# w3 x w_out on merged words as native float32 products, and a planner that books GpSimd and VectorE together

## The chip, the core and the metric

The kernel runs on one NeuronCore of a Trainium2 chip. In the views PE is TensorE, PEld its weight load, DVE VectorE, ACT ScalarE, POOL GpSimd, and SP the engine that issues the DMAs. The metric is the device time of one execution in microseconds: the kernel before takes 945.75 us (median of 3 runs, 943.49 to 945.9). The profile comes from one execution of its own, of 944.89 us, with a span of 943.1 us from its first to its last instruction.

## The reference, cut to what matters

Attention over 4 batches, 8 heads, 576 positions and 64 columns a head, with a window of 128 positions and a slope for each head, feeds two dense layers over the 2304 tokens:

```
scores = where(0 <= i - j < 128, q @ k.T / 8 - slope * |i - j|, -1e9)
x = softmax(scores) @ v                     # 2304 x 512
x = ((x @ w1) * (x @ w2)) @ w3 @ w_out      # w1, w2: 512x1024; w3: 1024x1024; w_out: 1024x512
x = relu(x @ w_in) ** 2 @ w_out2            # w_in: 512x2048; w_out2: 2048x512
```

The activations are float32; all weights come as float64, as pairs of 32-bit words.

## The kernel before, in words

**Weights.** A weight tile is 128 rows of 1024 float64 numbers (1 MB), loaded by `w_load` (L253) into a tile `raw` of 128 x 1024 x 2 words. Four passes turn each pair into one float32 word that stands in the place of the low word: `conv_g` (L266) scales the high word, `conv_s` (L270) shifts the low one, and `conv_m` (L281, twice, on DVE alone) merges them. Two more passes split the merged word for TensorE: `conv_hi` (L288) copies it as fp32r, `conv_lo` (L299) subtracts the copy from the word; both halves go to a tile `wu`. A product of two such operands is `mm3` (L155): three fp32r products (high x high, high x low, low x high, L156 to L158). There are 36 tiles: 4 of w_out (`wo`), 8 of w3, 8 of w1 and w2 (`w12`) and 16 of the last layer (`w2`).

**W34.** Before any token passes, `p_w34` (L700) forms w3 x w_out in 64 steps (8 rows of blocks, 8 blocks of the inner sum each), each step one `mm3` of 128 x 512 from a w3 tile and half of a `wo` tile into PSUM tile `g`. `l_w34h` and `l_w34l` split the result. All 64 steps must be done before the tiles of the gated layer are opened (`gp`, L875).

**Heads.** A head (`add_head`, L603) goes through load, scaling or splitting of q and k, `p_qk` (ten score products, tile `s`), `l_min` (L406, DVE, from PSUM), `l_exp` (ACT), `l_sum` (DVE, small), `l_norm` (L439, any of three engines), transposes `p_tr1`, `p_tr2` (tile `t`), a copy of them (`l_pth`), and the product with v, `p_pva` and `p_pvb` (tiles `a`, `b`). Heads in `NQ` (the first 9) have native float32 score products, heads in `NV` (the first 12) native float32 products with v; the others take split operands. A native product of N columns runs as two passes over its N columns, which the views count as two instructions. Two heads make one 128-row block of x, split by `t_xh` and `t_xl` in two halves of 288 tokens.

**Gated layer.** For each batch and half, `p_ab` (L743) makes two up-projections of 12 products of 288 columns for each of 8 blocks; `l_a` (ACT) copies the first, `l_gf` (L756, DVE) multiplies by the second, `l_gh` and `l_gl` split the gate (tile `gt`). `p_y` multiplies by W34. All heads but those of the first batch are worked in between. The last layer follows after the planned part, in a fixed order (`r_step`, `o_step`, from L910).

**What sets the order.** `Plan.run` (L52) is a list scheduler. Each task has a rank, a price on each engine that can take it, what it waits for, and the buffers that it takes and gives back. The planner takes the earliest start and, among tasks that can start then, the lowest rank; a task goes to the engine where its end plus a bias (L37) is lowest. What it writes down is each engine's instruction order; on the chip every engine works through its own list in that order and waits by semaphores. In the kernel before, each engine is booked for itself.

## Time and profile before

| | |
|---|---|
| time, median of 3 runs | 945.75 us (943.49 to 945.9) |
| the profiled execution | 944.89 us, span 943.1 us |
| busy over the span | PE 905.7, DVE 470.6, ACT 420.5, POOL 325.9 us |
| until the first up-projection starts | 145.49 us |
| from there to the first product of the last layer | 394.3 us |
| the last layer | 403.3 us |

A matmul's duration in the views includes the time in which it runs through the array, so a busy PE is not the same as a full PE: what a product costs in a dense stretch is read from the distance between two starts. The views give an instruction's wall time, with the time in which it was held up after its start in it.

### The profile page before, as it was taken

What the parts mean: (1) busy time and instruction counts of PE and PEld (TensorE: products, weight loads), DVE (VectorE), ACT (ScalarE), POOL (GpSimd) and SP (SyncE); (2) the same over time, 40 slices, a digit from 0 to 9 for tenths busy, and PEclk for the clock granted to TensorE, in tenths of its full rate; (3) what the DMA queues carried; (4) which work ended last, traced back from release to release, by engine and by line L of the source; (5) the groups of instructions that cost most, each with busy time, mean ns of one, the idle gap of its engine ahead of it and who ended that gap; (6) DMA issues with size and microseconds to landing.
All of it is one profiled execution on the core that took longest, in us unless ns stands there. A gap on an engine that the chain in (4) does not pass through costs nothing.

```text
span 943.1 us, 13950 instructions
## 1 busy us (share of the span) xinstructions
PE 905.7 (96%) x5248; PEld 791.0 (84%) x5248; DVE 470.6 (50%) x981; ACT 420.5 (45%) x955; POOL 325.9 (35%) x354
## 2 busy tenths in 40 slices
PE   5699988999999999999999999999999999999998
PEld 3466657899999999999999978888888888888897
DVE  5969969667676665417313995231223122212222
ACT  4566667667777666434323353232223222222222
POOL 6887988766656655336323200000000000000000
PEclk9899999999999999999999999999999999999999
DMA  7647542233332322025006541020002000100010
GB/s 228 216 159 244 169 135 83 64 98 82 74 83 65 105 66 63 7 72 195 31 7 210 177 146 48 0 74 17 1 1 79 0 1 8 49 0 1 1 46 23
DMA packets 31075, 73.74 MB, mean 78 GB/s; under 512 B 5792, under 2 KB 14496, under 8 KB 26912
## 3 DMA queue, kind: packets, MB, share of 16 engines
q1 hardware_dynamic: 31008, 72.86, 25.2%
q8 instruction: 41, 0.67, 0.3%
q14 instruction: 26, 0.21, 0.1%
HBM read 63.41 MB, written 9.44 MB: 77 GB/s over the span
## 4 chain that ended last, share of the span: by engine, by line
PE 79%; DVE 10%; POOL 5%; issue 3%; DMA 2%; ACT 1%; SPq 0%; POOLq 0%; DVEq 0%; ACTq 0%
PE g L156 9%; PE g L158 9%; PE g L157 9%; PE o L157 7%; PE o L158 7%; PE o L156 7%; PE r L157 7%; PE r L158 7%; PE r L156 7%; DVE raw L283 5%; POOL e L197 2%; PE s L447 2%; PE s L450 1%; PE s L449 1%; PE t L470 1%
## 5 line engine op out<-in xcount | busy, mean ns | idle before, releaser
L921 ACT ACTIVATE t<-r 128x512 f32<-128x512 f32 (+1 forms) x80 | 44.4, 555 | 258.7 <-PE r L158 258.7
L923 DVE CAST rr<-s 128x512 fp32r<-128x512 f32 (+1 forms) x80 | 32.0, 400 | 250.9 <-ACT s L922 250.8
L156 PE MATMUL g<-x,wu 128*128 128x288 f32 x512 | 153.7, 300 | 0.6 <-DVE gf L758 0.6
L157 PE MATMUL g<-x,wu 128*128 128x288 f32 x512 | 151.8, 297 | 0.0
L158 PE MATMUL g<-x,wu 128*128 128x288 f32 x512 | 151.5, 296 | 0.0
L157 PE MATMUL r<-ys,wu 128*128 128x512 f32 (+1 forms) x320 | 118.9, 371 | 0.0
L158 PE MATMUL r<-ys,wu 128*128 128x512 f32 (+1 forms) x320 | 118.8, 371 | 0.0
L156 PE MATMUL r<-ys,wu 128*128 128x512 f32 (+1 forms) x320 | 118.6, 371 | 0.0
L157 PE MATMUL o<-wu,rr 128*128 128x512 f32 x288 | 113.3, 393 | 0.0
L156 PE MATMUL o<-wu,rr 128*128 128x512 f32 x288 | 112.9, 392 | 0.0
L158 PE MATMUL o<-wu,rr 128*128 128x512 f32 x288 | 112.8, 392 | 0.1
L283 DVE SCALAR_TENSOR_TENSOR raw<-raw 128x1024 uint32<-128x1024 uint32 x72 | 109.1, 1517 | 1.5 <-POOL raw L197 0.4
L156 PEld LDWEIGHTS g<-x,wu 128*128 128x128 f32 x512 | 96.9, 189 | 0.9 <-DVE gf L758 0.9
L157 PEld LDWEIGHTS g<-x,wu 128*128 128x128 f32 x512 | 97.5, 190 | 0.0
L158 PEld LDWEIGHTS g<-x,wu 128*128 128x128 f32 x512 | 97.3, 190 | 0.0
L164 POOL TENSOR_TENSOR gt<-gf,gt 128x288 fp32r<-128x288 f32 x61 | 57.9, 951 | 99.4 <-ACT gt L161 98.9
L197 POOL TENSOR_SCALAR e<-e,st 128x256 f32<-128x256 f32 (+1 forms) x115 | 76.9, 684 | 23.7 <-DVE st L437 14.5
L156 PE MATMUL g<-gt,wu 128*128 128x288 f32 x256 | 76.6, 299 | 0.5 <-DVE gf L758 0.5
L157 PE MATMUL g<-gt,wu 128*128 128x288 f32 x256 | 75.9, 296 | 1.0 <-POOL gt L164 1.0
L158 PE MATMUL g<-gt,wu 128*128 128x288 f32 x256 | 75.5, 295 | 0.0
L758 DVE TENSOR_TENSOR gf<-g,a_sb 128x288 f32<-128x288 f32 x64 | 29.1, 454 | 83.9 <-PE g L158 83.8
L156 PEld LDWEIGHTS r<-ys,wu 128*128 128x128 f32 x320 | 60.2, 188 | 11.6
(123 smaller groups left out, 1863.0 us busy)
## 6 DMA issues: line engine op xcount, KB each, us to landing
raw<-in_w2io_dram SPq DMA_DIRECT2D x16, 1024.0 KB, 4.9
qkraw<-in_qk_dram SPq DMA_DIRECT2D x46, 288.0 KB, 4.3
raw<-in_w3t_dram SPq DMA_DIRECT2D x8, 1024.0 KB, 7.5
raw<-in_w_dram SPq DMA_DIRECT2D x8, 1024.0 KB, 5.1
y_scr<-ye SPq DMA_DIRECT2D x32, 144.0 KB, 1.7
out_dram<-ob SPq DMA_DIRECT2D x18, 256.0 KB, 2.1
raw<-in_w_out_dram SPq DMA_DIRECT2D x4, 1024.0 KB, 6.2
yr<-y_scr SPq DMA_DIRECT2D x16, 256.0 KB, 2.8
```

What stands on the lines that cost most here:

```text
L156: nc.tensor.matmul(o, wh, xh, start=start, stop=False)
L157: nc.tensor.matmul(o, wh, xl, start=False, stop=False)
L158: nc.tensor.matmul(o, wl, xh, start=False, stop=stop)
L164: eng.tensor_tensor(out=o, in0=a, in1=b, op=ALU.subtract)
L197: nc.gpsimd.tensor_scalar(out=o, in0=i, scalar1=c, scalar2=1.0, op0=ALU.mult, op1=ALU.mult)
L283: nc.vector.scalar_tensor_tensor(out=low, in0=high, scalar=(3, 0x80000000)[part], in1=low, op0=(ALU.logical_shift_left, ALU.bitwise_and)[p ...
L447: nc.tensor.matmul(o, qb, d["kh"][:, k0:k1], start=True, stop=True)
L449: nc.tensor.matmul(o, qb, d["kh"][:, k0:k1], start=True, stop=False)
L450: nc.tensor.matmul(o, qb, d["kl"][:, k0:k1], start=False, stop=True)
L758: nc.vector.tensor_tensor(out=t, in0=ab.pop((b, hf, fi, 1)), in1=ab.pop((b, hf, fi, 2)), op=ALU.mult)
L921: nc.scalar.activation(out=t, in_=o, func=ACTF.Relu)
L923: nc.vector.tensor_copy(out=rr[:, 0, 0:n], in_=s)
```

## The change

1. The split of the 12 `wo` and w3 tiles goes: the new `add_words` has the load and the four passes that merge, and `add_weights` adds the split for `w12` and `w2` alone. `p_w34` multiplies the merged words themselves, where they stand (every second word of `raw`), as one native float32 product of 128 x 512 for three fp32r ones. The `wo` words are loaded into the pool `su`.
2. The planner knows a second name for DVE, `D`: work of DVE that reads two operands from SBUF, or copies or scales from SBUF to SBUF. `D` and POOL's work are booked one at a time (`lock`). Reads of PSUM and the small sums stay `d`.
3. `NV` goes from 12 heads to 7, ranks and biases have new numbers, and a start may be up to 0.1 later for a lower rank (`LOOK`).
4. The first w3 tile is loaded before the first `wo` tile, and four native products of 256 columns of constants stand at the head of TensorE's list (`p_warm`).

```diff
--- before.py
+++ after.py
 NQ = frozenset(range(9))
-NV = frozenset(range(12))
-RANK = dict(w34=6.0, h0=-4.0, w12=85.0, w12s=10.0, w12l=10.0)
+NV = frozenset(range(7))
+RANK = dict(w34=6.25, h0=-10.7, w12=37.2, w12s=7.96, w12l=9.7)
...
-    LOOK = 0.0
-    bias = dict(d=1.75, a=0.7, p=0.0)
+    LOOK = 0.1
+    bias = dict(d=3.0, D=0.34, a=0.3, p=0.0)
...
+        lock = 0.0
...
                 best = None
-                for e, w in where.items():
+                for q, w in where.items():
+                    e = q.lower()
                     t = max(t0, free.get(e, 0.0))
+                    if q in "Dp":
+                        t = max(t, lock)
                     for d in deps:
                         t = max(t, end[d] + (0.0 if on[d] == e else self.lat[on[d]]))
-                    key = t + w + self.bias.get(e, 0.0)
+                    key = t + w + self.bias.get(q, 0.0)
                     if best is None or (key, t) < best[:2]:
-                        best = (key, t, e, w)
+                        best = (key, t, q, w)
...
-            t, rank, n, e, w = min(near, key=lambda c: (c[1], c[0], c[2]))
+            t, rank, n, q, w = min(near, key=lambda c: (c[1], c[0], c[2]))
+            e = q.lower()
...
             fin = t + w
             end[n], on[n] = fin, e
-            free[e] = t + (w if e != "dma" else w)
+            free[e] = fin
+            if q in "Dp":
+                lock = fin
...
     def w_copy(n, ps=False):
-        return {"a": 0.2 + n * 0.00094, "d": 0.2 + n * (0.0011 if ps else 0.0006)}
-
-    def w_tt(n, engs="dp"):
-        w = {"d": 0.15 + n * 0.00106, "p": 0.22 + n * 0.0023}
+        return {"a": 0.2 + n * 0.00094, "d" if ps else "D": 0.2 + n * (0.0011 if ps else 0.0006)}
+
+    def w_tt(n, engs="Dp"):
+        w = {"d": 0.15 + n * 0.00106, "D": 0.15 + n * 0.00106, "p": 0.22 + n * 0.0023}
         return {e: w[e] for e in engs}
 
-    def w_ts(n, engs="dap"):
-        w = {"d": 0.16 + n * 0.00053, "a": 0.2 + n * 0.00094, "p": 0.35 + n * 0.0009}
+    def w_ts(n, engs="Dap"):
+        w = {"D": 0.16 + n * 0.00053, "a": 0.2 + n * 0.00094, "p": 0.35 + n * 0.0009}
         return {e: w[e] for e in engs}
 
...
     def w_load(key):
         kind, i = key
         src = {"wo": w_out, "w3": w3t, "w12": w12, "w2": w2io}[kind]
-        t = wp.tile([128, 1024, 2], U32, tag="u", bufs=10, name="raw")
+        if kind == "wo":
+            t = su.tile([128, 1024, 2], U32, tag="v", bufs=4, name="raw")
+        else:
+            t = wp.tile([128, 1024, 2], U32, tag="u", bufs=10, name="raw")
...
         kind, i = key
-        if kind == "wo":
-            u = su.tile([128, 2, 1024], F32R, tag="v", bufs=4, name="wu")
-        elif kind == "w2" and i < 4:
+        if kind == "w2" and i < 4:
             u = w2_pool[0].tile([128, 2, 1024], F32R, tag="v", bufs=4, name="wu")
         else:
             u = slot("u34" if kind == "w2" and i >= 12 else "u")
...
+    def add_words(key, rank, tag, users, keep, lead):
+        k = "%s%d" % key
+        hold("raw" + k, tag, users)
+        add("ld" + k, rank - lead, {"dma": w_dma(1048)}, lambda e: w_load(key), takes=["raw" + k], keep=keep)
+        add("cg" + k, rank, w_ts(1024), lambda e: conv_g(key, e), ["ld" + k])
+        add("cs" + k, rank, w_ts(1024, "Da"), lambda e: conv_s(key, e), ["ld" + k])
+        add("cm" + k, rank, {"D": 1.23}, lambda e: conv_m(key, e, 0), ["cg" + k, "cs" + k])
+        add("cn" + k, rank, {"D": 1.23}, lambda e: conv_m(key, e, 1), ["cm" + k])
+
     def add_weights(key, rank, users, tag="u", keep=1, deps=(), lead=0.0):
         k = "%s%d" % key
-        hold("raw" + k, "u", 2)
+        add_words(key, rank, "u", 2, keep, lead)
         hold("w" + k, tag, users)
-        add("ld" + k, rank - lead, {"dma": w_dma(1048)}, lambda e: w_load(key), takes=["raw" + k], keep=keep)
-        add("cg" + k, rank, w_ts(1024), lambda e: conv_g(key, e), ["ld" + k])
-        add("cs" + k, rank, w_ts(1024, "da"), lambda e: conv_s(key, e), ["ld" + k])
-        add("cm" + k, rank, {"d": 1.23}, lambda e: conv_m(key, e, 0), ["cg" + k, "cs" + k])
-        add("cn" + k, rank, {"d": 1.23}, lambda e: conv_m(key, e, 1), ["cm" + k])
-        add("ch" + k, rank, w_copy(1024), lambda e: conv_hi(key, e), ["cn" + k, *deps], takes=["w" + k])
-        add("cl" + k, rank, w_tt(1024), lambda e: conv_lo(key, e), ["ch" + k], gives=["raw" + k])
-
-        plan.tasks["ch" + k] = plan.tasks["ch" + k][:5] + (("raw" + k,),) + plan.tasks["ch" + k][6:]
+        add("ch" + k, rank, w_copy(1024), lambda e: conv_hi(key, e), ["cn" + k, *deps], ["w" + k], ["raw" + k])
+        add("cl" + k, rank, w_tt(1024), lambda e: conv_lo(key, e), ["ch" + k], [], ["raw" + k])
...
+    def p_warm():
+        t = ps_t.tile([128, 512], F32, tag="t", name="t")
+        for _ in range(4):
+            nc.tensor.matmul(t[:, 0:256], ident, bm, start=True, stop=True)
+
+    hold("warm", "t", 1)
+    add("warm", -100.0, {"pe": 5.0}, lambda e: p_warm(), [], ["warm"], ["warm"])
     add("ptz1", 0.0, {"p": 0.5}, lambda e: new_pt(True))
...
-            add(f"kl{n}", r, {"d": 0.76}, lambda e: t_kl(n, e), N("kh"), [], R)
+            add(f"kl{n}", r, {"D": 0.76}, lambda e: t_kl(n, e), N("kh"), [], R)
...
     def p_w34(fi, c):
         if c == 0:
             gw[fi] = ps_g.tile([128, 512], F32, tag="g", name="g")
-        wl = ws["w3", fi][:, :, c * 128:(c + 1) * 128]
-        wr = ws["wo", c // 2][:, :, (c % 2) * 512:(c % 2) * 512 + 512]
-        mm3(gw[fi], wl[:, 0], wl[:, 1], wr[:, 0], wr[:, 1], c == 0, c == 7)
+
+        wl = f(raws["w3", fi][:, c * 128:(c + 1) * 128, 0])
+        wr = f(raws["wo", c // 2][:, (c % 2) * 512:(c % 2) * 512 + 512, 0])
+        nc.tensor.matmul(gw[fi], wl, wr, start=c == 0, stop=c == 7)
...
         for c in range(8):
             k = f"ww{fi}_{c}"
             add(
-                k, 1000 + rank + 0.01 * c, {"pe": 3 * w_mm(512)}, lambda e, c=c: p_w34(fi, c),
-                [f"chw3{fi}", f"clw3{fi}", f"chwo{c // 2}", f"clwo{c // 2}"] + ([f"ww{fi}_{c - 1}"] if c else []),
-                [f"gw{fi}"] if c == 0 else [], [f"ww3{fi}"] + ([f"wwo{c // 2}"]),
+                k, 1000 + rank + 0.01 * c, {"pe": w_nat(512)}, lambda e, c=c: p_w34(fi, c),
+                [f"cnw3{fi}", f"cnwo{c // 2}"] + ([f"ww{fi}_{c - 1}"] if c else []),
+                [f"gw{fi}"] if c == 0 else [], [f"raww3{fi}", f"rawwo{c // 2}"],
             )
...
-    load_order = [("wo", 0), ("w3", 0), ("w3", 1), ("wo", 1), ("wo", 2), ("w3", 2), ("wo", 3)] + [("w3", i) for i in range(3, 8)]
+    load_order = [("w3", 0), ("wo", 0), ("w3", 1), ("wo", 1), ("wo", 2), ("w3", 2), ("wo", 3)] + [("w3", i) for i in range(3, 8)]
     for j, key in enumerate(load_order):
-        add_weights(key, RANK["w34"] * j, 16 if key[0] == "wo" else 8, "wo" if key[0] == "wo" else "u")
+        rank = RANK["w34"] * j
+        if key[0] == "wo":
+            add_words(key, rank, "wo", 16, 0, 0.0)
+        else:
+            add_words(key, rank, "u", 8, 1, 0.0)
     for i in range(8):
         add_weights(("w12", i), RANK["w12"] + RANK["w12s"] * i, 4 * B, lead=RANK["w12l"])
```

Three places show how the lists move. On PE, the steps of W34 whose `wo` tile is the first (`wu_187` before, `raw_155` after) and the work behind them:

```order
L156 MATMUL g_327<-wu_187,wu_275 128x512
L157 MATMUL g_327<-wu_187,wu_275 128x512
L158 MATMUL g_327<-wu_187,wu_275 128x512
L156 MATMUL g_327<-wu_187,wu_275 128x512
L157 MATMUL g_327<-wu_187,wu_275 128x512
L158 MATMUL g_327<-wu_187,wu_275 128x512
L447 MATMUL s_343<-kn_283,qn_282 128x192
```

The same two steps in the changed kernel, with what follows:

```order
L725 MATMUL g_346<-raw_155,raw_195 128x512 x2
L515 MATMUL a_360<-pt_125,vn_248 64x512
L515 MATMUL a_360<-pt_125,vn_248 64x256 x2
L537 MATMUL b_368<-pt_125,vn_248 64x192
L538 MATMUL b_368<-pt_125,vn_248 64x64
L458 MATMUL s_371<-kn_256,qn_255 128x192
L725 MATMUL g_283<-raw_215,raw_138 128x512
```

Two steps of three products each are two native products now, on tiles `raw`, and a head's product with v stands right behind them. On POOL, the last rows ahead of the first up-projection (it needs `wu_919` and `x0_1009`), before:

```order
L197 TENSOR_SCALAR p40_110<-p40_110,st_822 64x192
L164 TENSOR_TENSOR wu_919<-raw_613,wu_919 128x1024
L197 TENSOR_SCALAR raw_895<-raw_895 128x1024
L164 TENSOR_TENSOR wu_963<-raw_650,wu_963 128x1024
L164 TENSOR_TENSOR x0_1009<-xf_849,x0_1009 128x288
L164 TENSOR_TENSOR x1_1022<-xf_849,x1_1022 128x288
L197 TENSOR_SCALAR e_990<-e_990,st_991 128x128
```

And in the changed kernel, ahead of its first up-projection:

```order
L205 TENSOR_SCALAR e_695<-e_695,st_696 128x256
L205 TENSOR_SCALAR raw_710<-raw_710 128x1024
L205 TENSOR_SCALAR raw_798<-raw_798 128x1024
L172 TENSOR_TENSOR vs_816<-vraw0_106,vs_816 128x5x64
L582 TENSOR_TENSOR ta_843<-ta_843,xf_759 64x128
L172 TENSOR_TENSOR qs_751<-qkraw_686,qs_751 64x576
```

The subtractions into `wu` and `x0`, `x1` have left POOL. They stand on DVE, as do those of the gate. DVE in the first batch of the gated layer, before:

```order
L758 TENSOR_TENSOR gf_1409<-g_1366,a_sb_1380 128x288
L385 SCALAR_TENSOR_TENSOR kl_1419<-qkraw_1281,kh_1403 128x576
L164 TENSOR_TENSOR wu_1412<-raw_1099,wu_1412 128x1024
L758 TENSOR_TENSOR gf_1450<-g_1421,a_sb_1441 128x288
L419 ISA e_1457,st_1458<-s_1444,bm_98 128x128
```

DVE in the first batch in the changed kernel:

```order
L778 TENSOR_TENSOR gf_1358<-g_1320,a_sb_1333 128x288
L172 TENSOR_TENSOR pt_760<-t_1339,pt_760 128x512
L172 TENSOR_TENSOR wu_1361<-raw_901,wu_1361 128x1024
L172 TENSOR_TENSOR gt_1377<-gf_1358,gt_1377 128x288
L778 TENSOR_TENSOR gf_1402<-g_1364,a_sb_1380 128x288
```

Between two gates (`gf`) DVE now has the gate's own subtraction (`gt`) as well. Of the 64 gate subtractions POOL had 61 and has 3; of the 64 gate copies ACT had 63 and has 13. Ahead of the first up-projection POOL's list has 63 instructions (106 before), DVE's 209 (210), ACT's 149 (134).

## Rows read from the trace of the kernel before

**Rows 1.** The page: busy time of each engine.

```profile
PE 905.7 (96%) x5248; PEld 791.0 (84%) x5248; DVE 470.6 (50%) x981; ACT 420.5 (45%) x955; POOL 325.9 (35%) x354
```

**Rows 2.** Busy by stretch: us, PE, PEld, DVE, ACT, POOL, clock, DMA share, GB/s.

```profile
0.00:145.50 145.50, 119.29 (x493) 80.68 (x494) 115.86 (x228) 87.95 (x203) 118.18 (x107) 0.95 0.57 188
145.50:539.80 394.30, 387.02 (x2934) 380.93 (x2933) 231.23 (x541) 221.43 (x560) 207.75 (x248) 1.00 0.31 86
539.80:943.10 403.30, 399.37 (x1826) 329.34 (x1824) 123.52 (x214) 111.11 (x192) 0.00 (x0) 1.00 0.09 31
```

**Rows 3.** PE in order of time (start, duration): first up-projection; last product.

```profile
145.49 0.29 PE L156 MATMUL g<-x,wu 128*128 128x288 f32 x1
...
938.93 0.39 PE L158 MATMUL o<-wu,rr 128*128 128x512 f32 x1
```

**Rows 4.** Groups of DVE and POOL, 0 to 145.5 us: busy, mean ns | idle before.

```profile
L283 DVE SCALAR_TENSOR_TENSOR raw<-raw 128x1024 uint32<-128x1024 uint32 x37 | 60.0, 1624 | 1.1 <-POOL raw L197 0.4
...
L197 POOL TENSOR_SCALAR e<-e,st 128x256 f32<-128x256 f32 (+1 forms) x34 | 32.2, 960 | 12.9 <-DVE st L437 7.8 <-DVE st L434 2.7 <-ACT p L427 2.3
L164 POOL TENSOR_TENSOR wu<-raw,wu 128x1024 fp32r<-128x1024 f32 x11 | 29.5, 2678 | 5.2 <-DVE st L434 1.9 <-DVE wu L205 1.9 <-ACT wu L161 1.2
L197 POOL TENSOR_SCALAR raw<-raw 128x1024 f32<-128x1024 f32 x19 | 28.8, 1520 | 5.2 <-DMA raw<-in_w_out_dram 4.8
```

**Rows 5.** The same operations: DVE 560 to 640 us, POOL 400 to 500 us.

```profile
L283 DVE SCALAR_TENSOR_TENSOR raw<-raw 128x1024 uint32<-128x1024 uint32 x5 | 6.1, 1220 | 0.0
...
L164 DVE TENSOR_TENSOR wu<-raw,wu 128x1024 fp32r<-128x1024 f32 x3 | 3.7, 1226 | 0.7 <-ACT wu L161 0.6
...
L164 POOL TENSOR_TENSOR wu<-raw,wu 128x1024 fp32r<-128x1024 f32 x4 | 9.8, 2448 | 10.7 <-ACT wu L161 8.3 <-issue 2.4
...
L197 POOL TENSOR_SCALAR raw<-raw 128x1024 f32<-128x1024 f32 x1 | 1.1, 1130 | 0.0
```

**Rows 6.** Groups of ACT, 0 to 145.5 us.

```profile
L427 ACT ACTIVATE e<-e,st 128x256 f32<-128x256 f32 (+1 forms) x44 | 20.8, 476 | 7.3 <-DVE st L419 7.2
L161 ACT ACTIVATE wu<-raw 128x1024 fp32r<-128x1024 f32 x13 | 14.9, 1143 | 8.4 <-POOL wu L164 5.8 <-DVE raw L283 2.7
L273 ACT ACTIVATE raw<-raw 128x1024 uint32<-128x1024 uint32 x12 | 13.9, 1169 | 0.1
```

**Rows 7.** PE in order of time, 110 to 118 us.

```profile
110.19 0.39 PE L156 MATMUL g<-wu 128*128 128x512 f32 x1
110.41 0.40 PE L157 MATMUL g<-wu 128*128 128x512 f32 x1
...
112.24 0.27 PE L478 MATMUL t<-swap,p 128*128 128x128 f32 x1
112.35 0.27 PE L479 MATMUL t<-ident,p 128*128 128x128 f32 x1
...
114.97 1.94 PE L504 MATMUL a<-pt,vn 128*64 128x512 f32 x6
116.74 0.49 PE L526 MATMUL b<-pt,vn 128*64 128x192 f32 x2
...
117.41 0.66 PE L470 MATMUL t<-ident,e 128*128 128x128 f32 x4
```

**Rows 8.** PE in order of time, a split head's products with v.

```profile
217.73 0.41 PE L509 MATMUL a<-pt,vs 128*128 128x512 f32 x1
...
218.99 0.32 PE L156 MATMUL g<-x,wu 128*128 128x288 f32 x1
```

**Rows 9.** PE in order of time: the same eight score passes, twice.

```profile
41.78 3.57 PE L447 MATMUL s<-kn,qn 64*128 64x192 f32 x8 [6.16 <-DVE kn L199]
...
97.71 1.88 PE L447 MATMUL s<-kn,qn 64*128 64x192 f32 x8 [0.40 <-DVE st L419]
```

**Rows 10.** Busy in two stretches, as Rows 2.

```profile
40.00:45.00 5.00, 3.22 (x8) 2.47 (x8) 4.81 (x11) 0.45 (x1) 4.68 (x5) 0.50 0.37 157
...
145.50:212.10 66.60, 62.38 (x446) 58.18 (x445) 49.51 (x120) 44.63 (x116) 52.06 (x57) 0.97 0.33 84
```

More of the change, by code (lines that the diff above doesn't have):

```diff
@@ L617, in add_head @@
             add(f"ldq{n}", r, {"dma": w_dma(295)}, lambda e: t_load_qk(n), [f"ldq{n - 1}"] if n else [], H_("qk"))
-            add(f"kn{n}", r, w_ts(576, "dap"), lambda e: t_kn(n, e), N("ldq"))
+            add(f"kn{n}", r, w_ts(576, "Dap"), lambda e: t_kn(n, e), N("ldq"))
             qd = N("kn")
```

## The prediction

> **What bounds the kernel now.** I read the page's busy times first [rows 1]: PE is busy for 905.7 of 943.1 us, nearly twice as long as any other engine. Then the stretches [rows 2, 3], because a busy PE can be a waiting chain early and a full array later. From 145.5 us to the end PE is busy for 786.4 of 797.6 us, and nothing that the other engines do there is worth more than the 11 us left. Before 145.5 us, the head phase, PE is busy for 119.3 us, and DVE with 115.9 and POOL with 118.2 us are as full as it is. The groups of that phase say why [rows 4, 5]: a merge on DVE takes 1624 ns there and 1220 ns where POOL stands idle, POOL's scaling of a weight tile takes 1520 ns against 1130, and its subtraction 2678 against 2448. DVE and POOL hold each other up. Over 37 merges that is 37 x 0.404 = 15 us of DVE, over 19 scalings 19 x 0.39 = 7.4 us of POOL. So the time is the start of the first up-projection, 145.5 us, and a tail of 797.6 us that PE fills.
>
> **The sum is made against the profiled execution**: span 943.1 us, 944.89 us in all, so 1.8 us lie around the span. The median of 945.75 is 0.9 us more, less than the runs differ among themselves.
>
> **The change, part by part, in the head phase.**
>
> *W34 on PE.* 192 fp32r products go, of 0.22 to 0.23 us from start to start [rows 7]: 43 us. 64 native products come, each two passes over 512 columns. The head's product with v shows native passes: two of 512 and four of 256 columns, 2048 in all, take 116.74 - 114.97 = 1.77 us [rows 7], so 1024 columns take 0.885 us and 64 products 56.6 us. Bounds: 0.46 us each if a pass ran like an fp32r one (29 us), 1.77 us each if reading every second word halves the rate (113 us; a rival below). I take 0.885, the only native row.
>
> *Products with v.* Five heads go from native, 117.41 - 114.97 = 2.44 us [rows 7], to split, 218.99 - 217.73 = 1.26 us [rows 8]: -5.9 us on PE over the whole kernel, for two more subtractions a head on DVE.
>
> *What PE must do before the first up-projection in the changed list.* 64 products 56.6; scores of 9 native heads at 1.88 us for eight of their passes [rows 9], so about 2.26 for ten, 20.3; nine transposes of 0.11 us for each of 9 heads [rows 7], 8.9; 7 native products with v 17.1 and 2 split ones 2.5; part of a split head's scores, 1. Together 106 us. The list before, with ten heads and 192 products, comes to 100 by the same prices, and took 145.5. The other 45 us were waits and half clock: at 40 to 45 us the granted clock is 0.50 [rows 10], which is 1.2 of 2.4 GHz, after PE had stood idle for 6.16 us, and there the same eight score passes take 3.57 us against 1.88 [rows 9].
>
> *DVE.* 36 merges stand ahead of the first up-projection. At the quiet price that is 43.9 us. The rest of its phase before was 115.9 - 60.0 = 55.9 us. A subtraction of 1024 columns takes 1.23 us there in quiet [rows 5], so I price one of 288 at 0.4 and one of 512 at 0.65 us: eight for x, four for the first split heads and a few copies are about 7 us more; four shifts and one head's minima are about as much less. Sum 100 us. *POOL* loses all 11 weight subtractions (29.5 us), 19 of 34 normalisations of `e` (18.2) and 7 of 19 scalings (10.6), with the subtractions of x: 118.2 falls to about 50 at the held-up prices. *ACT* loses 10 weight copies at 1.14 us, gains 12 shifts at 1.17 and 16 normalisations at 0.48 [rows 6]: 88.0 - 11.4 + 14.0 + 7.7 = 98 us.
>
> *The start.* So three engines need 106, 100 and 98 us, where before DVE and POOL filled 116 and 118 and lost another 27 to 30 to waits. None can end before about 107. If DVE loses 30 us again, or PE its 26 of idle time [rows 2], it is 130 to 132. The booking of DVE and POOL and the shorter path to a step of W34 (no copy and subtraction of 1.14 and 2.68 us between merge and product) speak for less; three engines that are equally full speak for more than a quarter of it. I take 120 us: DVE's 100 and 20 us of filling and waits. The four warm-up products cost between 4 x 2 x 0.45 = 3.6 us at half clock and -1.7 us (3.57 - 1.88), if the first scores then run at 2.4 GHz; constants and PE stand idle there until the first load lands, so I take 0. The loading order of the first two tiles moves a wait of PE that the head's own chain hides; 0.
>
> *The tail.* One head more is left after the start: scores about 1.2, transposes 1.0; its products with v: 23 x 1.26 against 2 x 2.44 + 20 x 1.26, -1.1. Together +1 us on PE. The holes of the first half batch, 66.6 - 62.4 = 4.2 us [rows 10], sit behind POOL's subtractions of x and weights, which are gone from there; I count half back, -2. DVE takes 58 gate subtractions and some 50 gate copies from POOL and ACT, 108 x 0.4 = 43 us by the price above, over a stretch in which it is busy for 231 of 394 us and PE has no hole [rows 2]: hidden, as long as DVE's 274 us stay spread. Where they bunch, in the first two batches, each gate that comes late holds a PSUM tile; with two such waits of 0.5 us in each of 16 blocks that is 16 us at worst, a later first tile of the next batch included.
>
> Sum: 120 + 797.6 + 1 - 2 = 916.6 us of span, 918 with what lies around it; I forecast 917.
>
> **The rivals.**
>
> *A. The waits stay.* The booking is a planner's matter. On the chip each engine works through its list when its operands are there, and two lists that drift by a microsecond meet again. For it: the small sums (`st`) are not booked, and three full engines wait for one another. Against it: POOL has 43 of 106 instructions fewer there, so there is less to meet. Then PE keeps its 26 us of idle time, start 132 us, and DVE's bunched gates add 4 to 8: 132 + 797.6 + 1 + 6 + 1.8 = 938 us, or 930 with no such gates.
>
> *B. Not what it says.* If the head phase hangs on the chain of each head (scores, minima, exponentials, normalisation, transposes, product) and not on full lists, relief on POOL buys nothing and the longer products pay for themselves: start 143 to 147, 941 to 946 us. For it: PE waits for POOL's and DVE's scaling of k, steps of the chain. Against it: DVE and POOL were each busy for over 115 us of the 145.5, which a pure chain wouldn't do.
>
> *C. Slower: the strided words.* The native products read both operands with a step of 8 bytes; nothing in the trace has PE read with a step. If a pass runs at half rate there, a product costs 1.77 us, PE's sum is 106 + 64 x 0.885 = 163, and with the 14 us of gaps that I grant the start is 177 us: 177 + 797.6 + 1 + 1.8 = 977 us. It decides from the point where the start passes 146: (146 - 14 - 49.4) / 64 = 1.29 us a product. Against it: ACT's copy of 1024 merged words, read with the same step, takes 1143 ns, 1.1 ns a word, while its 256 neighbouring ones take 476 ns, 1.9 ns each with the fixed part [rows 6]: there the step costs nothing that can be seen.
>
> The Trainium skill (SBUF — State Buffer, section "SBUF: two separate sides") says that a reader keeps its full rate as long as at least two accesses fall into each 16-byte line, and pays for each line beyond that; with 8 bytes from word to word that holds just so. By it this rival's price falls away, a product keeps 0.885 us, and C would have 0.04 at most; as no row here shows PE with a step, C keeps the 0.09 that one row of another engine leaves it.
>
> **How the numbers follow.** The forecast has 0.62 (start 110 to 130, so 905 to 928 us); A 0.21 (928 to 940); B 0.08 (940 to 947); C 0.09. The range takes the forecast's lower bound, start 107 and tail holes closed (107 + 797.6 - 7 + 1.8, about 899), and A's upper end, 940; outside lie B, C and what little is left below, 2 in 10. A measurement can tell about 0.3% (2.8 us) from no change. Faster: the forecast, A and half of B, 0.87. Same: 0.05. Slower: C and a remainder of B, 0.08.
>
> **What would show it.** The first up-projection starts at 110 to 130 us in the changed trace; the tail from there is within 8 us of 797.6; a merge on DVE in the head phase is nearer 1220 than 1624 ns, and POOL's busy time there is near 45 us. Two starts of native products on `raw` lie 0.43 to 0.45 us apart at full clock (two such passes a product); 0.85 or more apart would be rival C. A start at 130 or later with DVE and POOL idle for more than 30 us each would be A or B, and PE holes before the gates of the first two batches would show DVE as the new bound. The forecast is wrong if the start comes before 105 or after 132, or if the tail moves by over 10 us.

## The result: 920.3 us, and the profile after

The changed kernel takes 920.32 us (median of 4 runs, 919.21 to 921.40) against 944.76 for the kernel before (4 runs on the same chip, 943.49 to 945.90): 0.9742 of the time, 95% interval 0.9722 to 0.9761. The forecast was 917 with a range of 899 to 940. In the profiled executions the span falls from 943.1 to 919.6 us.

The first two lines are from the page of the changed kernel: busy time of each engine, to be read beside [rows 1], and the shares of the chain that ended last. The third is the chain of the kernel before.

```profile
PE 908.6 (99%) x5192; PEld 777.8 (85%) x5192; DVE 515.7 (56%) x1189; ACT 417.5 (45%) x941; POOL 115.7 (13%) x166
...
PE 92%; DVE 4%; issue 1%; DMA 1%; ACT 1%; POOL 0%; SPq 0%; DVEq 0%; POOLq 0%; ACTq 0%
```

```profile
PE 79%; DVE 10%; POOL 5%; issue 3%; DMA 2%; ACT 1%; SPq 0%; POOLq 0%; DVEq 0%; ACTq 0%
```

PE does about as much as before and is now the chain almost alone (92% of it for 79%). POOL has lost two thirds of its work, DVE has 45 us more. The three stretches that answer to [rows 2]:

```profile
0.00:127.80 127.80, 123.45 (x405) 65.50 (x406) 95.68 (x213) 90.09 (x197) 41.25 (x62) 1.00 0.60 203
127.80:515.90 388.10, 385.74 (x2966) 383.18 (x2965) 295.78 (x765) 216.03 (x552) 74.46 (x104) 1.00 0.32 91
515.90:919.60 403.70, 399.42 (x1826) 329.16 (x1824) 124.28 (x215) 111.34 (x193) 0.00 (x0) 1.00 0.09 31
```

The head phase is 17.7 us shorter (127.8 for 145.5), the batches 6.2 (388.1 for 394.3), and the last layer is the same. In the head phase PE is idle for 4.4 us where it was for 26.2, and DVE, ACT and POOL each have more than 30 us to spare there: PE is the bound, not one of them. PE in order of time (start, duration), with the first of the rows that answer to [rows 9], two runs of native W34 passes, and the row that answers to [rows 3]:

```profile
3.36 3.78 PE L614 MATMUL t<-bm,ident 128*128 128x256 f32 x8 [3.36 <-POOL bm L196]
7.07 4.21 PE L458 MATMUL s<-kn,qn 64*128 64x192 f32 x10
11.51 3.57 PE L458 MATMUL s<-kn,qn 64*128 64x192 f32 x8 [0.23 <-DVE st L430]
...
59.72 3.88 PE L725 MATMUL g<-raw 128*128 128x512 f32 x8
63.53 0.59 PE L458 MATMUL s<-kn,qn 64*128 64x192 f32 x2
...
127.83 0.29 PE L164 MATMUL g<-x,wu 128*128 128x288 f32 x1
```

Head 0's scores come 1.7 us later than in the trace before (7.07 for 5.33), behind the warm-up, and head 1's eight passes still take 3.57 us, as at [rows 9]'s low clock. Yet the granted clock of that stretch reads 1.00, where it read 0.50 in [rows 10]:

```profile
10.00:15.00 5.00, 4.77 (x12) 3.14 (x11) 3.33 (x16) 4.22 (x13) 1.49 (x4) 1.00 0.94 312
```

Eight W34 passes take 63.53 - 59.72 = 3.81 us with the switch behind them. Over all 128 the median from start to start is 0.451 us.

Groups of DVE and POOL, 0 to 127.8 us, beside [rows 4, 5]:

```profile
L294 DVE SCALAR_TENSOR_TENSOR raw<-raw 128x1024 uint32<-128x1024 uint32 x36 | 47.3, 1318 | 0.6
...
L205 POOL TENSOR_SCALAR raw<-raw 128x1024 f32<-128x1024 f32 x13 | 17.6, 1359 | 18.5 <-DMA raw<-in_w3t_dram 9.7 <-DMA raw<-in_w_dram 7.4 <-DMA raw<-in_w_out_dram 1.4
L205 POOL TENSOR_SCALAR e<-e,st 128x256 f32<-128x256 f32 (+1 forms) x15 | 8.7, 592 | 28.7 <-DVE st L445 9.7 <-DVE st L448 9.0 <-ACT raw L284 7.8
```

A merge takes 1318 ns (1624 before, 1220 in quiet), and POOL's normalisation 592 (960 before).

**A count for all runs.** In each trace I took the time from every PE product to the next start. For one kind of product and number of columns there is a usual value, the one that a third lie below. The sum of the usual values over all products is PE's work; what lies above it is waiting, half rate and switches from one kind of product to another. (The eight warm-up passes all run slowly, so their 3.7 us count as work.) Before: 870.6 of work and 63.0 above it (from the first start at 5.33 to the last at 938.93 us). After: 881.6 and 30.5, starting 2.0 us earlier. So PE got 11.0 us more work and lost 32.5 us of what lies above it: 11.0 - 32.5 - 2.0 = -23.5, the difference of the spans.

### The profile page after: what moved, and what is told of

It reads as the page before. It is cut to its first block, busy times and chain, and to the rows that moved or that the text cites. A ratio compares the mean times of both kernels' runs of the same rounds, so it can differ in the third digit from the quotient of the medians.

```text
span 919.6 us, 13785 instructions
## 1 busy us (share of the span) xinstructions
PE 908.6 (99%) x5192; PEld 777.8 (85%) x5192; DVE 515.7 (56%) x1189; ACT 417.5 (45%) x941; POOL 115.7 (13%) x166
## 4 chain that ended last, share of the span: by engine, by line
PE 92%; DVE 4%; issue 1%; DMA 1%; ACT 1%; POOL 0%; SPq 0%; DVEq 0%; POOLq 0%; ACTq 0%
PE g L164 9%; PE g L166 9%; PE g L165 9%; PE o L165 7%; PE o L166 7%; PE o L164 7%; PE r L165 7%; PE r L166 7%; PE r L164 7%; PE g L725 7%; PE s L458 3%; PE t L481 2%; PE a L515 2%; PE s L461 1%; PE s L460 1%; DVE raw L294 1%
## 5 line engine op out<-in xcount | busy, mean ns | idle before, releaser
L294 DVE SCALAR_TENSOR_TENSOR raw<-raw 128x1024 uint32<-128x1024 uint32 x72 | 91.7, 1277 | 2.3 <-ACT raw L284 1.4
L164 PEld LDWEIGHTS r<-ys,wu 128*128 128x128 f32 x320 | 60.2, 188 | 11.7
L165 PEld LDWEIGHTS r<-ys,wu 128*128 128x128 f32 x320 | 60.2, 188 | 11.5
L166 PEld LDWEIGHTS r<-ys,wu 128*128 128x128 f32 x320 | 60.1, 188 | 11.0
L438 ACT ACTIVATE e<-e,st 128x256 f32<-128x256 f32 (+1 forms) x128 | 60.5, 475 | 17.0 <-DVE st L430 16.7
```

The costliest lines, as they stand in the source:

```text
L164: nc.tensor.matmul(o, wh, xh, start=start, stop=False)
L165: nc.tensor.matmul(o, wh, xl, start=False, stop=False)
L166: nc.tensor.matmul(o, wl, xh, start=False, stop=stop)
L294: nc.vector.scalar_tensor_tensor(out=low, in0=high, scalar=(3, 0x80000000)[part], in1=low, op0=(ALU.logical_shift_left, ALU.bitwise_and)[p ...
L438: nc.scalar.activation(out=e, in_=e, func=ACTF.Exp, bias=st[:, 0, i:i + 1], scale=-1.0, accum_out=st[:, 1, i:i + 1],)
```

## The experiments

| run | us | ratio to before | PE work | above it |
|---|---|---|---|---|
| changed kernel | 920.3 | 0.9742 (0.9722 to 0.9761) | 881.6 | 30.5 |
| no warm-up task | 931.4 | 0.9849 (0.9836 to 0.9862) | 878.0 | 42.5 |
| no booking | 949.7 | 1.0038 (1.0026 to 1.0050) | 881.1 | 55.2 |
| split W34 | 944.3 | 0.9988 (0.9978 to 0.9998) | 866.5 | 67.7 |
| native W34 alone | 942.5 | 0.9973 (0.9960 to 0.9987) | 882.0 | 50.7 |
| warm-up booked, not issued | 920.5 | 0.9734 (0.9721 to 0.9746) | 878.5 | 31.1 |
| no warm-up, ranks again | 919.4 | 0.9723 (0.9710 to 0.9735) | 876.9 | 31.7 |
| split W34, ranks again | 935.7 | 0.9897 (0.9871 to 0.9923) | 867.7 | 60.9 |
| more work on POOL | 940.3 | 0.9947 (0.9932 to 0.9962) | 882.5 | 45.8 |
| booking in the head phase | 944.1 | 0.9989 (0.9978 to 1.0000) | 880.6 | 53.7 |
| booking in the batches | 929.0 | 0.9829 (0.9808 to 0.9849) | 880.0 | 38.3 |
| 8 heads with native scores | 918.9 | 0.9723 (0.9706 to 0.9741) | 876.7 | 31.0 |
| 6 heads with native v | 916.2 | 0.9690 (0.9672 to 0.9707) | 875.7 | 29.7 |

The ratio is to runs of the kernel before on the same chip, whose medians lie from 944.7 to 946.0 us. The work differs by at most 16 us among them, and what lies above it by 38. All edits are to the changed kernel unless another is named; `...` marks lines of an edit that are left out.

**No warm-up task.**

```
-    hold("warm", "t", 1)
-    add("warm", -100.0, {"pe": 5.0}, lambda e: p_warm(), [], ["warm"], ["warm"])
```

> The changed kernel without the four warm-up products. Theory (the warm-up buys nothing: in the changed trace head 0's scores start at 7.07 us instead of 5.33, and the scores of head 1 at 11.5 us still take 3.57 us for eight passes, the price at the clock of 1.2 GHz): head 0 starts about 1.7 us earlier, the full clock comes at the same 20 to 22 us, the first up-projection starts 0 to 2 us earlier than 127.8, time 918 to 921 us against 920.3. Rival (the warm-up brings the full clock forward, from 22.2 us before to 20.5 us after, and PE now sets the start): without it the full clock comes 1.7 us later, some of PE's work of 14 to 22 us runs at half rate longer, start 129 to 132 us, time 922 to 925 us.

931.4 us, outside both. The planner saw PE free 5 us sooner and wrote another list from head 1 on. The first up-projection started earlier, at 125.0 us, but the list broke 30 us later. Its stretch from 150 to 175 us, and PE's longest wait there:

```profile
150.00:175.00 25.00, 21.67 (x140) 20.57 (x139) 20.82 (x54) 14.71 (x41) 3.74 (x5) 0.86 0.25 59
```

```profile
PE g L164 <- DVE wu L213: 2.2, 1, 2.2
```

PE stops for a weight copy that DVE reaches late, and the granted clock falls below 1 in the same stretch. By the count, 7 of the 12 us that this run has more above PE's work stand in it. The next two runs separate the warm-up from the list.

**Warm-up booked, not issued.**

```
     def p_warm():
-        t = ps_t.tile([128, 512], F32, tag="t", name="t")
-        for _ in range(4):
-            nc.tensor.matmul(t[:, 0:256], ident, bm, start=True, stop=True)
+        return
```

> The changed kernel with the warm-up still booked in the planner but no warm-up product issued: every engine's list is that of the changed kernel, instruction by instruction, less eight matmul passes. Theory (the warm-up itself buys nothing; the run without it in the planner lost 11 us because the planner wrote another list, whose holes stand at 150 to 175 us): 917 to 921 us, head 0 starts about 1.7 us earlier. Rival (the matmuls themselves bring the clock forward and are worth the 11 us): 928 to 933 us.

920.5 us, as the theory had it. PE in order of time:

```profile
4.89 4.20 PE L458 MATMUL s<-kn,qn 64*128 64x192 f32 x10 [4.89 <-DVE kn L207]
9.32 3.56 PE L458 MATMUL s<-kn,qn 64*128 64x192 f32 x8 [0.23 <-DVE st L430]
```

Every engine's list is that of the changed kernel. Head 0 starts 2.2 us sooner, and the passes are as slow as behind the warm-up. The warm-up matmuls are worth nothing; what the run without the task lost is the list.

**No warm-up, ranks chosen again.** The two lines of the task go as in the first run, and:

```
-RANK = dict(w34=6.25, h0=-10.7, w12=37.2, w12s=7.96, w12l=9.7)
+RANK = dict(w34=6.43, h0=-11.66, w12=38.57, w12s=8.45, w12l=8.54)
```

> The changed kernel without the warm-up task, with the five ranks chosen again for the list that the planner writes without it (w34 6.43, h0 -11.66, w12 38.57, w12s 8.45, w12l 8.54). Theory (what counts is whether the list fits, and ranks chosen for one list do not fit another): the 11 us come back, 917 to 923 us. Rival (the warm-up is needed): 928 to 933 us as without it before.

919.4 us: the 11 us come back by five numbers. Two lists of the same planner with the same work are 12 us apart, and any run here that changes the list may carry such a difference beside its own effect.

**Split W34.** The words become high and low tiles again and a product three fp32r ones:

```
...
-        nc.tensor.matmul(gw[fi], wl, wr, start=c == 0, stop=c == 7)
+        mm3(gw[fi], wl[:, 0], wl[:, 1], wr[:, 0], wr[:, 1], c == 0, c == 7)
...
```

> The changed kernel with W34 made again of three fp32r products on split tiles: 12 copies and 12 subtractions of 1024 columns come back, and PE loses 64 x (0.90 - 0.68) = 14 us. Planner with booking, 7 native heads and warm-up stay. Theory (relief of VectorE and GpSimd by the native products is the larger part of the gain): 12 subtractions cost 14.8 us on VectorE at 1.23, or 29 us and more on GpSimd with VectorE held meanwhile, so VectorE with 96 us goes to 110 and beyond and is the bound again, start 134 to 142 us, time 926 to 935 us. Rival (PE's own sum sets the start, the native products are only its longest term): start 112 to 122 us, time 904 to 914 us. A second rival (the planner alone carried the gain): same as the changed kernel, 918 to 923 us.

944.3 us, 9 beyond the theory's upper end. Part of it was ranks that did not fit, so the run was made again with five others:

```
-RANK = dict(w34=6.25, h0=-10.7, w12=37.2, w12s=7.96, w12l=9.7)
+RANK = dict(w34=5.65, h0=-10.69, w12=47.04, w12s=6.8, w12l=4.81)
```

> The changed kernel with W34 of three fp32r products on split tiles again, and the five ranks chosen again for that list (w34 5.65, h0 -10.69, w12 47.04, w12s 6.8, w12l 4.81). Theory (the native products' relief of the engines beside PE is worth something of its own, about half of the gain): 930 to 937 us, with over 10 us of PE waits left before 150 us. Rival (the 24 us lost by going back to split products were only ranks that did not fit): 918 to 925 us. Second rival (native W34 is the whole gain): 941 to 946 us.

935.7 us, as the theory had it. The stretch from 25 to 130 us, and the longest waits of PE before 150 us:

```profile
25.00:130.00 105.00, 93.11 (x365) 61.22 (x364) 88.90 (x170) 77.33 (x160) 30.29 (x36) 0.89 0.57 195
```

```profile
PE t L488 <- ACT pt L169: 4.7, 3, 3.1
PE t L480 <- ACT e L209: 3.8, 1, 3.8
```

PE has 13.9 us less work than in the changed kernel (867.7 for 881.6) and 30.4 us more above it. It waits for late results of ACT (copies of transposes, a normalisation) and of DVE, and the granted clock of the stretch is 0.89. That they are late because the 12 copies and 12 subtractions stand in their lists again is argued, not shown row by row. Native W34 under the new planner is worth 935.7 - 920.3 = 15 us, as far as both sets of ranks fit equally well: by waits that it takes away and against its own price on PE.

**Native W34 alone**, in the kernel before. Its planner, ranks and twelve native products with v stay, and only W34 is made as in the changed kernel, with the loads and merges that it needs:

```
...
-        mm3(gw[fi], wl[:, 0], wl[:, 1], wr[:, 0], wr[:, 1], c == 0, c == 7)
+        nc.tensor.matmul(gw[fi], wl, wr, start=c == 0, stop=c == 7)
...
```

> The kernel before with nothing but the native W34 on merged words: its planner without booking, its ranks, 12 heads with native products with v, no warm-up. Theory (native W34 takes 29.5 us of subtractions off GpSimd and about 11 us of copies off ScalarE; PE pays 14 us and five more native heads): the head phase is bound by PE or by VectorE at a held-up merge of 1450 to 1600 ns, start 132 to 140 us, time 930 to 938 us, about half of the gain of 24 us. Rival (the planner's booking and ranks carry the gain): start 143 to 150 us, time 942 to 948 us. Second rival (native products alone are the whole gain): start 126 to 130 us, time 919 to 923 us.

942.5 us: the theory's 930 to 938 is wrong, and the time is in the first rival's 942 to 948. The start is in neither range: it comes at 153.4 us, later than before. By then PE has started 489 instructions, where the changed kernel has 405 by its own start, so more of the heads is done ahead of it, and the batches take 385.3 us for 394.3. The merge, 0 to 130 us, and the stretch to 125 us:

```profile
L286 DVE SCALAR_TENSOR_TENSOR raw<-raw 128x1024 uint32<-128x1024 uint32 x34 | 53.0, 1559 | 6.5 <-ACT raw L276 4.9 <-POOL raw L197 0.4 <-issue 0.2
```

```profile
0.00:125.00 125.00, 111.70 (x385) 59.02 (x386) 95.79 (x212) 77.04 (x191) 85.81 (x98) 0.97 0.60 198
```

POOL is still busy for 86 us and the merge held up at 1559 ns. This kernel's ranks were not chosen again, so its gain of under 3 us may be too small by some of those 12.

**No booking.**

```
-                    if q in "Dp":
-                        t = max(t, lock)
```

> The changed kernel whose planner no longer books GpSimd's work and VectorE's two-operand work as excluding each other; costs, ranks, native products and warm-up stay. Theory (native W34 relieves GpSimd of 29.5 us, the booking is a planner's matter that the chip does not see): the planner gives GpSimd some work back, its busy time before the first up-projection rises from 41 to 50-65 us, a merge on VectorE takes 1320 to 1450 ns, but PE stays the bound of the head phase (busy 123 of 128 us), start 126 to 131 us, time 918 to 924 us. Rival (the booking is what took the waits away): the merge goes back to near 1600 ns, VectorE is full again and PE waits for it, start 135 to 142 us, time 928 to 936 us.

949.7 us, worse than either expected, and not where the rival had it. (The profiled execution took 945.7 us, the fastest of ten.) Busy by stretch, first of the changed kernel, then without booking:

```profile
0.00:125.00 125.00, 120.65 (x386) 63.18 (x387) 93.86 (x209) 88.68 (x194) 41.25 (x62) 1.00 0.60 206
125.00:425.00 300.00, 298.23 (x2304) 295.66 (x2303) 231.12 (x664) 189.43 (x508) 73.17 (x103) 1.00 0.28 69
```

```profile
0.00:125.00 125.00, 119.42 (x391) 61.62 (x392) 112.04 (x230) 73.02 (x165) 61.02 (x67) 0.96 0.63 215
125.00:425.00 300.00, 280.77 (x2116) 271.61 (x2115) 251.97 (x704) 164.38 (x451) 62.05 (x74) 1.00 0.26 65
```

To 125 us PE loses 1.2 us of busy time. The first up-projection even starts 4.4 us sooner, at 123.4 us, though DVE and POOL hold each other up more there. The merge before that start, and the batches from it to the last layer:

```profile
L292 DVE SCALAR_TENSOR_TENSOR raw<-raw 128x1024 uint32<-128x1024 uint32 x36 | 52.2, 1455 | 0.7
```

```profile
123.40:540.20 416.80, 396.95 (x2989) 386.99 (x2988) 338.28 (x841) 194.94 (x509) 76.53 (x83) 1.00 0.29 83
```

A merge takes 1455 ns for the changed kernel's 1318, and this costs nothing that the start shows. The whole loss lies in the batches, 416.8 us for 388.1. From 125 to 425 us PE does 2116 products where it did 2304, with DVE fuller by 21 us and ACT emptier by 25. The DVE groups of 125 to 425 us, changed kernel and then without booking, say what DVE does with the time:

```profile
L172 DVE TENSOR_TENSOR gt<-gf,gt 128x288 fp32r<-128x288 f32 x44 | 23.3, 529 | 1.5
L778 DVE TENSOR_TENSOR gf<-g,a_sb 128x288 f32<-128x288 f32 x48 | 21.9, 455 | 15.9 <-PE g L166 14.0 <-ACT e L209 1.0 <-PE s L460 0.4
...
L213 DVE CAST gt<-gf 128x288 fp32r<-128x288 f32 x35 | 12.7, 364 | 1.2
...
L207 DVE TENSOR_SCALAR e<-e,st 128x128 f32<-128x128 f32 x14 | 4.0, 286 | 0.5
```

```profile
L170 DVE TENSOR_TENSOR gt<-gf,gt 128x288 fp32r<-128x288 f32 x40 | 23.6, 589 | 1.4
L776 DVE TENSOR_TENSOR gf<-g,a_sb 128x288 f32<-128x288 f32 x41 | 18.6, 454 | 4.2 <-PE g L164 2.4 <-ACT a_sb L167 1.0 <-ACT e L436 0.3
L211 DVE CAST gt<-gf 128x288 fp32r<-128x288 f32 x40 | 18.4, 459 | 1.4
...
L205 DVE TENSOR_SCALAR e<-e,st 128x128 f32<-128x128 f32 (+1 forms) x39 | 14.7, 412 | 0.8
...
L205 DVE TENSOR_SCALAR p<-p,st 64x192 f32<-64x192 f32 x15 | 5.7, 377 | 0.5
```

Two things fill DVE. The larger is work that the planner gives it: 54 normalisations of `e` and `p` for 14, 20.4 us for 4.0. The other is longer instructions. The multiplication that reads PSUM (`gf`, from `g`) costs the same in both, while the gate's copy and subtraction, whose operands all lie in SBUF, grow by 95 and 60 ns. Summed over the whole batches, about 28 us of DVE's 44 us more are more tasks and 16 are longer ones. A copy in the changed kernel, and then one without booking, DVE in order of time and last POOL:

```profile
135.22 0.31 DVE L213 CAST gt<-gf 128x288 fp32r<-128x288 f32 x1
```

```profile
256.67 0.45 DVE L776 TENSOR_TENSOR gf<-g,a_sb 128x288 f32<-128x288 f32 x1
257.16 1.43 DVE L211 CAST gt<-gf 128x288 fp32r<-128x288 f32 x1
258.62 0.46 DVE L170 TENSOR_TENSOR gt<-gf,gt 128x288 fp32r<-128x288 f32 x1
```

```profile
256.99 1.42 POOL L170 TENSOR_TENSOR qs<-qkraw,qs 64x576 fp32r<-64x576 f32 x1 [7.91 <-PE a L522]
```

The copy that takes 0.31 us in the first row begins here while POOL subtracts, ends 0.18 us after POOL does (at 258.41), and shows 1.43 us. The Trainium skill (SBUF — State Buffer, section "SBUF: two separate sides") describes this as a lock on a port pair that one of the two engines holds for a whole instruction; this copy agrees, and so does the PSUM reader, whose mean stays at 454 to 456 ns in every run. The chain by line in the stretch from 125 to 425 us shows what grew out of it:

```profile
by line: DMA qkraw<-in_qk_dram 21.0%; issue 8.5%; DVE kl L394 5.2%; DVE gt L211 4.7%; DVE gf L776 4.0%; DVE xf L593 3.7%; DVE e L205 3.7%; DVE gt L170 3.6%; DVE pt L170 3.5%; SPq L359 3.3%; PE g L163 2.6%; PE g L162 2.6%; PE g L164 2.6%; DV
```

There is one buffer for raw q and k. Its next load starts when `kl` on DVE has read it, takes some 4.5 us, and then the head's conversions follow. With DVE full, `kl` comes late, and each head's load with it. In the changed kernel this load has 3.1% of the chain in the same stretch. (Taking that wait away with a second buffer was not tried.)

**Booking in one phase.** The planner books only before, or only after, 125 us of its own time:

```
-                    if q in "Dp":
+                    if q in "Dp" and lock < 125.0:
```

> The changed kernel whose planner books GpSimd and VectorE's two-operand work as excluding each other only before 125 us of its own time, that is in the head phase. Theory (the booking is worth its 29 us in the batches: without it anywhere the first up-projection started no later, at 123.4 us, and 31 us more of PE waits stood between 125 and 425 us): the batches lose again, 935 to 948 us. Rival (the booking works in the head phase, and the later holes followed from its list): 919 to 926 us.

```
-                    if q in "Dp":
+                    if q in "Dp" and lock > 125.0:
```

> The changed kernel whose planner books GpSimd and VectorE's two-operand work as excluding each other only after 125 us of its own time, in the batches of the mixture. Theory (the booking is worth its 29 us there): most comes back, 920 to 930 us, the rest being ranks that fit a little less. Rival (it works in the head phase): 938 to 950 us.

944.1 and 929.0 us, both as the theory had it. The batches with booking in the head phase alone, and with booking there alone:

```profile
125.00:425.00 300.00, 284.61 (x2136) 277.60 (x2136) 250.27 (x713) 166.43 (x456) 58.13 (x70) 0.99 0.28 70
```

```profile
125.00:425.00 300.00, 294.18 (x2259) 290.80 (x2258) 236.50 (x675) 183.54 (x495) 72.35 (x102) 0.99 0.28 71
```

The first has DVE at 250 us and 168 products fewer than the changed kernel, the second 236 and 45 fewer. Booking only in the head phase loses 24 of the 29 us, twice what the two lists above differ by. The 9 us that the other one loses are within that difference, so whether booking also helps in the head phase stays open.

**More work on POOL**, behind each of its tasks past 130 us of the plan, into a tile that nobody reads:

```
...
             plan.tasks[n][2](e)
+            if e == "p" and t0 > 130.0:
+                for _ in range(2):
+                    nc.gpsimd.tensor_tensor(out=junk, in0=ident, in1=ident, op=ALU.subtract)
```

> The changed kernel with every list as it is, and after each of GpSimd's 94 tasks past the head phase two more subtractions on GpSimd of 128 columns from a constant tile into a tile that nobody reads: some 75 us of work in time that GpSimd has free there (it is busy for 74 of 388 us). Theory (GpSimd's work holds VectorE's operations whose operands all lie in SBUF, and what the booking saves in the batches is this): VectorE's subtractions gt of 288 columns go from 529 to 600-700 ns on the average, its casts from 364 to 430 ns and more, PE gets holes of 3 to 15 us in the batches, 923 to 936 us. Rival (a free engine costs nothing; what the unbooked list lost was only the share that it gave to VectorE): 919 to 922 us, the durations as they were.

940.3 us: 20 us lost by work in POOL's idle time, with the list unchanged. The rival is out, and the theory's time was too small by 4. Three views of 125 to 425 us, POOL's group, PE's two longest waits and two DVE groups:

```profile
L925 POOL TENSOR_TENSOR junk<-ident 128x128 f32<-128x128 f32 x190 | 88.9, 468 | 9.3
```

```profile
PE t L482 <- POOL e L206: 8.9, 5, 4.5
PE t L490 <- DVE pt L172: 3.6, 3, 1.8
```

```profile
L172 DVE TENSOR_TENSOR gt<-gf,gt 128x288 fp32r<-128x288 f32 x40 | 22.8, 569 | 1.4
...
L214 DVE CAST gt<-gf 128x288 fp32r<-128x288 f32 x31 | 11.1, 358 | 1.0
```

The durations that the theory named were too large: the subtraction 569 ns for 600 to 700, the copy 358 for 430, no longer than before. `kl`, which reads SBUF alone too, takes 926 ns for 825. Of PE's waits most are for POOL's own late normalisations. So the run shows that POOL's free time is not free, but only part of its cost comes by holding DVE; POOL's own late results cost at least as much.

**Fewer native heads**, without the warm-up task, ranks and biases chosen again with booking:

```
-NQ = frozenset(range(9))
+NQ = frozenset(range(8))
-RANK = dict(w34=6.25, h0=-10.7, w12=37.2, w12s=7.96, w12l=9.7)
+RANK = dict(w34=5.99, h0=-9.11, w12=37.26, w12s=8.42, w12l=7.74)
-    bias = dict(d=3.0, D=0.34, a=0.3, p=0.0)
+    bias = dict(d=3.37, D=0.72, a=0.28, p=0.48)
```

> No warm-up task, 8 heads with native scores instead of 9, 7 with native products with v, ranks (w34 5.99, h0 -9.11, w12 37.26, w12s 8.42, w12l 7.74) and biases (d 3.37, D 0.72, a 0.28, p 0.48) chosen again with booking. Theory (PE sets the end from 25 us on, so only less work on PE or fewer of its 17 us of waits before the last layer can help; one native head less takes about 1 us off PE): 916 to 920 us, a beat of the changed kernel by 1 to 4 us. Rival (fewer native heads load VectorE and ScalarE at the start, and the list loses there more than PE gains): 921 to 928 us.

```
-NV = frozenset(range(7))
+NV = frozenset(range(6))
-RANK = dict(w34=6.25, h0=-10.7, w12=37.2, w12s=7.96, w12l=9.7)
+RANK = dict(w34=6.72, h0=-10.02, w12=41.78, w12s=8.22, w12l=8.74)
-    bias = dict(d=3.0, D=0.34, a=0.3, p=0.0)
+    bias = dict(d=3.23, D=0.66, a=0.09, p=0.3)
```

> No warm-up task, 9 heads with native scores, 6 instead of 7 with native products with v, ranks (w34 6.72, h0 -10.02, w12 41.78, w12s 8.22, w12l 8.74) and biases (d 3.23, D 0.66, a 0.09, p 0.3) chosen again with booking. Theory: one native product with v less takes 1.2 us off PE, 916 to 920 us. Rival (the two more subtractions on VectorE and a different list cost more): 921 to 928 us.

918.9 and 916.2 us. The second beats both kernels, 0.9690 of the time before (0.9672 to 0.9707, which lies apart from the changed kernel's interval). Its stretches:

```profile
0.00:124.20 124.20, 117.81 (x397) 63.38 (x398) 92.62 (x203) 92.94 (x206) 45.06 (x64) 1.00 0.65 214
124.20:510.60 386.40, 385.52 (x2965) 383.03 (x2964) 274.14 (x702) 239.94 (x613) 75.52 (x109) 1.00 0.32 90
510.60:914.70 404.10, 399.69 (x1826) 329.07 (x1824) 124.45 (x215) 112.01 (x193) 0.00 (x0) 1.00 0.09 30
```

PE's work is 5.9 us less (875.7 for 881.6: the warm-up, one native product with v, the rest smaller), what lies above it 0.8 less, its first start some 1.8 later. The batches hold 0.9 us of PE's idle time; with PE this full, little but less work on it is left to gain there.

## Why the prediction was right, and where not

*W34 on PE: right.* A pass every 0.451 us is 0.90 us a product, 0.93 with the gaps (59.7 us for 64), where the forecast had 0.885. Rival C, half rate by the stride, is out. (The 476 ns that spoke against it at [rows 6] are a mean over two sizes of an exponential, not of a copy; 256 columns alone take 502, which leaves the argument as it was.)

*DVE, ACT, POOL in the head phase: right within 10% for two.* DVE has 95.7 and ACT 90.1 us where 100 and 98 were expected; POOL has 41.3, 17% under the expected 50.

*The start: 120 expected, 127.8 measured.* The step that failed is "DVE's 100 and 20 us of filling and waits". DVE was not the bound. PE's own sum was, which the prediction had at 106 us: 3.4 us before its first product, 3.7 of warm-up, 106 of work, and 14.7 above it, 8.1 of these in the first 25 us, mostly half rate, make the 127.8. Under rival C it had granted PE 14 us of gaps on its 106, which came out at 14.7; over half of them are no waits but the slow first 20 us, which it had cost at nothing. Its 106 + 14 leave out the 3.4 us before the first product and the warm-up's 3.7, of which little could be saved: without the warm-up products the start is 127.2. That DVE and POOL hold each other up is real, but did not set this start: without booking a merge takes 1455 ns, DVE is busy for 110 us, and the start comes at 123.4.

*The warm-up at 0: right* by the run that only leaves it out.

*The tail: 796.6 expected (797.6 + 1 - 2), 791.8 measured.* The term mis-sized is the holes of the batches, "-2": PE's idle time there went from 7.3 to 2.4 us, and its busy time fell by 1.3. By the count, PE's work from the start on is 0.9 us more, as the prediction's "+1" had it, and what lies above it 6.7 less. Two readings were wrong: [rows 2] show 394.30 - 387.02 = 7.3 us of idle time where the prediction saw "no hole", and its 4.2 us in the first half batch do not wait for subtractions of x and weights, but mostly for these two, a normalisation and a subtraction of q:

```profile
PE t L470 <- POOL e L197: 2.8, 2, 2.6
PE s L449 <- POOL qs L164: 1.1, 1, 1.1
```

DVE's extra work in the middle, 43 us by the prediction, was 64.6 (295.8 for 231.2) and is hidden, as expected, but only under the booking.

*The total: partly luck.* The start came 7.8 us later than forecast and the tail 4.8 us shorter, so the span of 919.6 lies only 3.0 us above the sum's 916.6.

*Rival A: its reason was wrong.* It said that a planner's booking doesn't reach the chip, and the prediction let the booking "speak for less". It reaches the chip as another list: what it changes most is how much work the planner gives DVE. Without it the gain is gone, and the loss lies in the batches. The head phase, where the whole argument looked, keeps its gain without the booking (start at 123.4 us); with it the batches take the work that moved to DVE in 388.1 us, without it in 416.8.

*What the prediction did not see is how much the list itself weighs.* Native W34 alone gave under 3 us, and planner, ranks, heads and warm-up without it 10 (ranks chosen again), but both together 24. That the parts do not add is not shown by this: the 11 us that are missing are no more than the 12 by which two lists of one rule differ, and the first of these runs kept ranks made for other work. Ranks for the kernel before with native W34, or for the unbooked planner, were not chosen again, so how much of their loss is the rule and how much the list is not settled beyond those 12 us. Nor was the kernel before run with new ranks alone, or with the 12 to 7 heads, the biases, `LOOK` or the loading order alone; what each of these gives stays open.

## What to carry to other kernels

Where two engines hold each other up, let the planner book the one while the other runs, and look for the effect over the whole list, not only where the page shows the fullest stretch: here it lay in the batches. Before an edit to a planned kernel is judged by its time, look whether it rewrote the list: run it once with the list as it was, and once with the order's numbers chosen again. An engine with much free time is not a free place, if what it finishes late, or what it holds, lies in another engine's chain.

## Not expected of the hardware

- Native float32 passes that read both operands with a step of 8 bytes run every 0.451 us for 512 columns in the median: against the 1.77 us for 2048 columns of [rows 7], 0.443 for 512, the step costs under 3%.
- In the first 20 us PE's passes run at half the later rate while the granted clock of the rows reads 1.00; matmuls issued from 3.36 us on change nothing (head 1's eight score passes: 3.57 us with them, 3.56 without, 1.88 later at [rows 9]).
- A 288-column copy on DVE took 1.43 us when it began during a subtraction on POOL, and 0.31 us when it began before one; the multiplication that reads PSUM kept a mean of 454 to 456 ns in every kernel.
